# The bias of the last 64 query rows: masks for two key blocks at once in an attention and MLP kernel

## The chip, the cores and the metric

One core of a Trainium2 chip runs the whole program. The metric is the device time of one execution in microseconds. Three runs of the kernel before took 797.27, 798.25 and 798.29 us; the median is 798.25 us.

## The reference

Attention with 4 batches, 8 heads, 576 positions and head size 64, with a bias that a small network makes of the distance, followed by a two-layer MLP on 2304 rows:

```
scores = scale * q @ k.T                      # (4, 8, 576, 576)
x      = log1p(|i - j|) / log1p(max(i, 1))
h      = relu(x * w1 + b1)                    # 32 hidden
bias   = h @ w2                               # one 576 x 576 table per head
attn   = softmax(scores + bias);  o = attn @ v
y      = relu(o @ w_in) ** 2 @ w_out          # 512 -> 2048 -> 512
```

The bias doesn't depend on the batch, so its 8 tables are computed once.

## The kernel before, in words

**Query chunks.** The 576 query rows are four chunks of 128 and a tail chunk of 64 (`TAIL = 4`). `chunks` puts the tail first. A unit of attention is a batch, a pair of heads `hp` and a chunk. In a tail unit the two heads of the pair share the 128 partitions: the even head's 64 rows below, the odd head's above. The first 8 units are the tail units of two batches, then come the units of chunks 0 to 3 of these batches, then the other two batches.

**The bias.** Each hidden unit is a ramp, so for a query row the bias over keys is a sum of slopes and offsets of those hidden units that are active. For a block of 32 keys (`jb`, 18 of them) and a chunk, `bias_mask` (L361) compares the distances with thresholds `theta` on VectorE (DVE): 128 partitions are 4 keys by 32 hidden units, the free axis 8 groups by 128 query rows, f16. `bias_sum` (L378) multiplies each of the 8 masks by `wmov`, which holds w1*w2 and b1*w2 in two f16 parts, into one PSUM bank `bb`: 128 rows, 8 groups x (slope or offset) x 8 heads x 4 keys. ScalarE (ACT) scales the offsets out of PSUM (L392, for the tail L403), DVE multiplies the slopes by `xc`, the chunk's matrix x (L393, L404), GpSimd (POOL) adds both into the table in SBUF (L398, L405).

**The tail before.** A mask holds the 64 tail rows twice, in the lower and upper 64 columns: by a window with a repeat (L373), or for the six blocks whose bit is set in `MD` by a half mask (L369) that ACT copies (L375). The product gives all 8 heads in both halves; then two half-height ACT and DVE instructions take the even heads from the lower 64 partitions and the odd heads from the upper ones (L403, L404). Each of the 18 blocks takes 16 matmuls.

**Attention.** `scores` (L410): PE makes 576 scores into `sp` (L428, one PSUM buffer); DVE adds the bias and takes the maximum in one instruction (L434) and frees `sp`; ACT exponentiates (L439). `transposes` and `values` follow (L484, L487, L502), with copies out of PSUM by ACT. The `bb` tiles share four PSUM buffers with these ("aux"), masks have three buffers (`MB`), and `xc` has two: the tail's and the next chunk's. `load_xc` (L114) issues the load from SP and then scales the matrix on ACT (L121).

**The order.** The program is written with due counts: `bias_upto(n)` works off the list of (chunk, block) items, `K0` and `B1` say how many are due between the loads of the first batch's heads, `BO` how many beside each unit. A scheduler then places the instructions of each engine by its own estimate of times; the order that results is fixed and each engine works through its own list. SP issues the loads: constants, the tail's xc, then k, q and v of eight (batch, pair) groups, seven loads each, and then the xc of chunk 0.

Of the kernel before, what the change touches and what calls it, by code (L numbers as in the profile page):

```python
# [79 lines left out]
def attention_then_relu2_mlp(ctx: ExitStack, tc: tile.TileContext, q, k, v, cols, w_in, w_out, psi, xmat, dist, out):  # L80
# [279 lines left out]

    def bias_mask(ic, jb):  # L361
        m = prep.tile([128, 8, 128], F16, name="mask", tag="mask", bufs=MB)
        dup = ic == TAIL and (MD >> jb) & 1
        w = 64 if dup else 128
        base = sdist[:, 128 * ic + 548 - 32 * jb:]
        if ic < TAIL or dup:
            win = bass.AP(tensor=base.tensor, offset=base.offset, ap=[base.ap[0], [4, 8], [1, w]])
            th = theta[:, 128 * ic:128 * ic + w].unsqueeze(1)
            DVE.tensor_tensor(out=m[:, :, :w], in0=win, in1=th.to_broadcast([128, 8, w]), op=ALU.is_ge)  # L369
# [8 lines left out]
    def bias_sum(ic, jb):  # L378
        m = mask_t.pop((ic, jb))
        bb = ps.tile([128, 512], F32, name="bb", tag="aux", bufs=4)  # L380
        for r in range(8):
# [4 lines left out]
        xv = xc_t[ic][:, 32 * jb:32 * jb + 32].rearrange("p (g j) -> p g j", j=4).unsqueeze(1)
        bv = bb.rearrange("p (g a h j) -> p a h g j", g=8, a=2, h=H)
        tv = t.rearrange("p h (g j) -> p h g j", j=4)
        sv = s.rearrange("p h (g j) -> p h g j", j=4)
        js = slice(32 * jb, 32 * jb + 32)  # L390
# [499 lines left out]
```

## Time and profile before

| | |
|---|---|
| median of three runs | 798.25 us |
| profiled execution, its own time | 797.97 us |
| its span | 796.2 us |
| PE busy | 723.5 us, 91% |
| DVE busy | 574.5 us, 72% |
| ACT busy | 456.5 us, 57% |
| POOL busy | 186.4 us, 23% |

The span runs from the first to the last instruction of the profile. PE is the tensor engine (PEld its weight loads), SP the engine that issues the DMAs. A busy PE isn't PE at its peak. In the chain of waits, the work that ended last followed backwards, PE has 50% of the span, DVE 19%, ACT 8%, DMA 7% and the issuing on SP 6%.

### The profile page before, as it was taken

How to read it: one execution, taken by the hardware profiler on the slowest of the kernel's cores; microseconds unless marked ns; L12 is line 12 of the kernel's file. 1: busy time of each engine (PE TensorE's matmuls, PEld its weight loads, DVE VectorE, ACT ScalarE, POOL GpSimd, SP SyncE). 2: the span in 40 equal slices, each digit the busy share in tenths (PEclk: the TensorE clock that was granted, in tenths of full speed). 3: DMA queues.
4: the chain of work that ended last, by engine and by line, in shares of the span. 5: the costliest groups of instructions: out<-in, count | busy, mean ns of one | idle time of the engine just before them, and what ended most of it. 6: DMA issues, size and time to landing. Idle time of an engine off the chain costs nothing.

```text
span 796.2 us, 17616 instructions
## 1 busy us (share of the span) xinstructions
PE 723.5 (91%) x7094; PEld 571.7 (72%) x7094; DVE 574.5 (72%) x1215; ACT 456.5 (57%) x940; POOL 186.4 (23%) x295
## 2 busy tenths in 40 slices
PE   5499999999988999979889899999989999999992
PEld 5456778787756676656677677878768887888881
DVE  7867778785666678898897979784845576557661
ACT  5757777777655678888676656664442233224220
POOL 1444333232210023342223324250400021000000
PEclk7869999999989999999999999999999999999997
DMA  7610000000376522301231143001010001000100
GB/s 203 191 60 18 3 16 2 3 2 2 105 239 232 189 85 85 111 28 54 80 107 54 67 146 107 28 22 59 26 54 1 1 1 54 1 1 1 54 2 27
DMA packets 27990, 50.14 MB, mean 63 GB/s; under 512 B 5252, under 2 KB 13444, under 8 KB 27908
## 3 DMA queue, kind: packets, MB, share of 16 engines
q1 hardware_dynamic: 27908, 49.01, 18.8%
q8 instruction: 56, 0.92, 0.5%
q14 instruction: 26, 0.21, 0.1%
HBM read 43.23 MB, written 5.77 MB: 62 GB/s over the span
## 4 chain that ended last, share of the span: by engine, by line
PE 50%; DVE 19%; ACT 8%; DMA 7%; SPq 6%; issue 5%; POOL 3%; DVEq 0%; ACTq 0%; POOLq 0%
PE y L766 16%; PE ha L717 8%; PE sp L428 7%; PE px L502 6%; PE hb L717 5%; PE pp L484 4%; PE bb L383 4%; DMA stage<-in_w_in 3%; DVE t L434 3%; ACT p L439 2%; SPq L150 2%; SPq L151 2%; DVE area L618 2%; DVE gl L747 1%; DVE wa L185 1%
## 5 line engine op out<-in xcount | busy, mean ns | idle before, releaser
L766 PE MATMUL y<-w,gh 128*128 128x512 f32 x576 | 177.9, 401 | 2.5 <-ACT gh L746 1.3
L717 PEld LDWEIGHTS <-area 128*128 128x128 f16 x1680 | 147.4, 99 | 42.5 <-issue 15.3
L439 ACT ACTIVATE p<-t,negm 128x576 f32<-128x576 f32 x144 | 111.2, 775 | 27.0 <-DVE negm L434 26.8
L434 DVE CUSTOM_DVE_ANT_0 t<-sp,area 128x576 f32<-128x576 f32 x144 | 104.1, 752 | 30.0 <-PE sp L428 21.3
L766 PEld LDWEIGHTS y<-w,gh 128*128 128x128 f32 x576 | 105.9, 190 | 24.9 <-ACT gh L746 2.9
L428 PE MATMUL sp<-k,q 64*128 64x288 f32 (+1 forms) x640 | 108.2, 447 | 15.0 <-DVE negm L434 11.4
L717 PE MATMUL ha<-area 128*128 128x256 f16 (+1 forms) x960 | 106.3, 266 | 9.0 <-DVE area L734 4.9
L766 PE MATMUL y<-w,gl 128*128 128x512 f32 x288 | 107.5, 397 | 1.1 <-DVE gl L747 1.1
L502 PE MATMUL px<-pt,v 128*64 128x128 f32 (+1 forms) x1600 | 96.6, 267 | 3.5 <-DVE xT L507 2.0
L485 ACT COPY pt<-pp 128x512 f32<-128x512 f32 x144 | 79.7, 582 | 32.0 <-PE pp L484 31.9
L502 PEld LDWEIGHTS px<-pt,v 128*64 128x64 f32 x1600 | 79.2, 137 | 19.7 <-issue 8.2
L484 PE MATMUL pp<-ident,p 128*128 128x128 f32 x576 | 84.5, 283 | 5.5 <-ACT pt L485 2.4
L428 PEld LDWEIGHTS sp<-k,q 64*128 64x128 f32 (+1 forms) x640 | 55.9, 182 | 41.1 <-DVE negm L434 15.3
L717 PE MATMUL hb<-area 128*128 128x256 f16 (+1 forms) x720 | 79.9, 262 | 1.4 <-DVE area L618 0.9
L484 PEld LDWEIGHTS pp<-ident,p 128*128 128x128 f32 x576 | 62.0, 142 | 22.8 <-issue 7.4
L398 POOL TENSOR_TENSOR area<-bt,bt 128x256 f32<-128x256 f32 x72 | 53.2, 763 | 81.9 <-DVE bt L393 81.9
L383 PE MATMUL bb<-wmov,mask 128*128 128x64 f16 x1440 | 52.6, 199 | 14.3 <-DVE bt L404 11.0
L766 PEld LDWEIGHTS y<-w,gl 128*128 128x128 f32 x288 | 53.8, 189 | 13.6 <-DVE gl L747 2.2
L383 PEld LDWEIGHTS <-mask 128*128 128x128 f16 x1440 | 48.2, 102 | 21.3 <-DVE bt L404 11.8
L369 DVE TENSOR_TENSOR mask<-sdist,theta 128x1024 f16<-128x1024 f16 (+1 forms) x78 | 49.7, 669 | 9.4 <-PE bb L383 9.4
L615 POOL TENSOR_TENSOR area<-xT 128x512 f32<-128x512 f32 (+1 forms) x17 | 22.8, 1344 | 143.2 <-DVE area L618 143.2
L747 DVE TENSOR_TENSOR gl<-area,gh 128x512 fp32r<-128x512 f32 (+1 forms) x40 | 30.2, 776 | 24.1 <-ACT gh L746 17.2
(153 smaller groups left out, 945.9 us busy)
## 6 DMA issues: line engine op xcount, KB each, us to landing
stage<-in_w_in SPq DMA_DIRECT2D x32, 512.0 KB, 4.2
stage<-in_w_out SPq DMA_DIRECT2D x16, 512.0 KB, 3.5
v<-in_v SPq DMA_DIRECT2D x16, 320.0 KB, 3.8
out<-o SPq DMA_DIRECT2D x18, 256.0 KB, 2.0
q<-in_q SPq DMA_DIRECT2D x32, 128.0 KB, 3.3
k<-in_k SPq DMA_DIRECT2D x16, 160.0 KB, 3.7
k<-in_k SPq DMA_DIRECT2D x16, 144.0 KB, 3.7
xc<-in_xmat SPq DMA_DIRECT2D x5, 288.0 KB, 3.6
```

The costliest lines, as they stand in the source:

```text
L369: DVE.tensor_tensor(out=m[:, :, :w], in0=win, in1=th.to_broadcast([128, 8, w]), op=ALU.is_ge)
L383: PE.matmul(bb[:, 64 * (7 - r):64 * (8 - r)], lhsT=m[:, r], rhs=wmov[:, n], start=(n == 0), stop=(n == 1))
L398: POOL.tensor_tensor(out=dst, in0=tw, in1=sw, op=ALU.add)
L428: mm = PE.matmul(out_t[to, x, :HALF], lhsT=qt[rows, cols], rhs=kt[rows, k0:k0 + HALF], start=True, stop=True)
L434: DVE.tensor_tensor_reduce(out=t.rearrange("p (x n) -> p x n", x=2), in0=sp[:, :, :HALF], in1=bias.rearrange("p (x n) -> p x n", x=2), sca ...
L439: ACT.activation(out=p[:, S * n:S * n + S], in_=t, func=AF.Exp, bias=negm[:, n:n + 1], scale=-1.0, accum_out=sums[:, 2 * ic + n:2 * ic + n ...
L484: PE.transpose(pp[:, 128 * c:128 * c + 128], p[:, k0:k0 + 128], ident)
L485: ACT.copy(pt[:, 4 * h:4 * h + 4], pp.rearrange("p (c m) -> p c m", c=4))
L502: PE.matmul(px[64 * h:64 * h + 64, :w], lhsT=vt[:, c, h], rhs=src, start=(c == 0), stop=(c == 4))
L717: PE.matmul(h[:, s, :w], lhsT=a, rhs=x, start=(k == 0), stop=(k == 5))
L747: DVE.tensor_tensor(out=gl, in0=g, in1=gh.bitcast(F32), op=ALU.subtract)
L766: PE.matmul(y, lhsT=a[:, slot, o:o + 128], rhs=x, start=((n, P) in firsts and f == 0 and m == 0), stop=((n, P) in lasts and f == 1 and m = ...
```

## The change

A mask of the tail now holds the 64 rows against two neighbouring key blocks, one in each half of its 128 columns (a window with a step of 32 in place of the repeat); `bias_mask` takes block pairs, 9 of them, and `MD` with its copies on ACT is gone. The weights `ab` are ordered with the even heads first. `bias_sum` multiplies each half of a mask by the even heads' weights into the lower 64 partitions and by the odd heads' into the upper ones, 64 rows by 32 columns each, 64 matmuls for a pair; then one ACT, one DVE and one POOL instruction of full height finish 64 keys. `K0`, `B1` and the calls of `bias_upto` count pairs in place of blocks. Chunks 0 to 3 are computed as before, with the heads' order put right in the view that POOL reads.

```diff
-B1 = (2, 13, 8)
+B1 = (2, 5, 8)
-MD = 37449
-K0 = 2
+K0 = 1
...
-            eng.tensor_scalar(out=ab[:, n], in0=col[:, 2:10], scalar1=(w1, b1)[n], scalar2=8.0, op0=ALU.mult, op1=ALU.mult)
+            eng.tensor_scalar(out=ab[:, n].rearrange("p (e h) -> p e h", e=2), in0=col[:, 2:10].rearrange("p (h e) -> p e h", e=2), scalar1=(w1, b1)[n], scalar2=8.0, op0=ALU.mult, op1=ALU.mult)
...
     def bias_mask(ic, jb):
...
-            win = bass.AP(tensor=base.tensor, offset=base.offset, ap=[base.ap[0], [4, 8], [0, 2], [1, 64]])
+            base = sdist[:, 128 * ic + 548 - 32 * (jb + 1):]
+            win = bass.AP(tensor=base.tensor, offset=base.offset, ap=[base.ap[0], [4, 8], [32, 2], [1, 64]])
             th = theta[:, 512:].unsqueeze(1).unsqueeze(1).to_broadcast([128, 8, 2, 64])
-            DVE.tensor_tensor(out=m.rearrange("p g (r i) -> p g r i", r=2), in0=win, in1=th, op=ALU.is_ge)
-        if dup:
-            ACT.copy(m[:, :, 64:], m[:, :, :64])
+            out = m.rearrange("p g (x i) -> p g x i", x=2)
+        DVE.tensor_tensor(out=out, in0=win, in1=th, op=ALU.is_ge)
...
     def bias_sum(ic, jb):
...
         else:
-            for r in range(2):
-                rows = slice(64 * r, 64 * r + 64)
-                bw = bb[rows].rearrange("p (g a h e j) -> p a e h g j", g=8, a=2, h=HP, e=2)
-                ACT.activation(out=sv[rows, :HP], in_=bw[:, 1, r], func=AF.Identity, scale=bscale[rows])
-                DVE.tensor_tensor(out=tv[rows, :HP], in0=bw[:, 0, r], in1=xv[rows].to_broadcast([64, HP, 8, 4]), op=ALU.mult)
-            POOL.tensor_tensor(out=bias_t[:, 8::9, js], in0=t[:, :HP], in1=s[:, :HP], op=ALU.add)
+            wv = wmov.rearrange("p n (a e y) -> p n e a y", a=2, e=2)
+            for x in range(2):
+                for r in range(8):
+                    o = 256 * x + 32 * (7 - r)
+                    for n in range(2):
+                        for e in range(2):
+                            PE.matmul(
+                                bb[64 * e:64 * e + 64, o:o + 32].rearrange("p (a y) -> p a y", a=2),
+                                lhsT=m[:, r, 64 - 64 * x:128 - 64 * x], rhs=wv[:, n, e], start=(n == 0), stop=(n == 1),
+                            )
+            xv = xc_t[ic][:, 32 * jb:32 * jb + 64].rearrange("p (g j) -> p g j", j=4).unsqueeze(1)
+            bv = bb.rearrange("p (g a h j) -> p a h g j", g=16, a=2, h=HP)
...
+            ACT.activation(out=sv.rearrange("p h (g j) -> p h g j", j=4), in_=bv[:, 1], func=AF.Identity, scale=bscale)
+            DVE.tensor_tensor(out=tv.rearrange("p h (g j) -> p h g j", j=4), in0=bv[:, 0], in1=xv.to_broadcast([128, HP, 16, 4]), op=ALU.mult)
+            POOL.tensor_tensor(out=bias_t[:, 8::9, 32 * jb:32 * jb + 64], in0=tv, in1=sv, op=ALU.add)
...
-    todo = [(ic, jb) for ic in chunks for jb in range(NJB)]
+    todo = [(ic, jb) for ic in chunks for jb in range(0, NJB, 2 if ic == TAIL else 1)]
...
-    bias_upto(NJB)
+    bias_upto(NJB // 2)
     load_xc(chunks[1])
...
-            bias_upto(NJB * (n + 1) + BO[r])
+            bias_upto(NJB // 2 + NJB * n + BO[r])
```

The lines of the new kernel are shifted: the scaling of xc is L120 there (L121 before), the tail's product, activation and add L411, L410 and L412, chunk 0's activation and product L388 and L389, the reduction L441 (L434), the exponential L446 (L439).

The scheduler also places other work anew. ACT at the end of the tail's bias, before (`bt` are the scaled offsets, `xc` the chunk's matrix, `p` the exponentials; in brackets the engines or load queues that a row waits for):

```order
L403 ACTIVATE bt_723<-bb,small 64x128 [waits DVE_49]
L392 ACTIVATE bt_788<-bb,small 128x256 [waits PE_49,Pool_49]
L392 ACTIVATE bt_812<-bb,small 128x256 [waits PE_49,Pool_49]
L439 ACT_TABLE_LOAD
L439 ACTIVATE p,sums<-t,negm 128x576 [waits DVE_49] x2
L121 ACTIVATE xc<-xc,small 128x576 [waits DMAHW4_49]
L439 ACTIVATE p,sums<-t,negm 128x576 [waits DVE_49]
L121 ACTIVATE xc<-xc,small 128x576 [waits DMAHW5_49]
L392 ACTIVATE bt_848<-bb,small 128x256 [waits PE_49,Pool_49]
```

And now the same place on ACT:

```order
L410 ACTIVATE bt_641<-bb,small 128x256 [waits PE_49,Pool_49]
L410 ACTIVATE bt_713<-bb,small 128x256 [waits PE_49,Pool_49]
L120 ACTIVATE xc<-xc,small 128x576 [waits DMAHW4_49]
L410 ACTIVATE bt_835<-bb,small 128x256 [waits PE_49,Pool_49]
L388 ACTIVATE bt_922<-bb,small 128x256 [waits PE_49,Pool_49]
L388 ACTIVATE bt_946<-bb,small 128x256 [waits PE_49,Pool_49]
L388 ACTIVATE bt_970<-bb,small 128x256 [waits PE_49,Pool_49]
L120 ACTIVATE xc<-xc,small 128x576 [waits DMAHW5_49,DVE_49]
L388 ACTIVATE bt_1006<-bb,small 128x256 [waits PE_49,Pool_49]
L446 ACT_TABLE_LOAD
L446 ACTIVATE p,sums<-t,negm 128x576 [waits DVE_49]
```

The scaling of chunk 0's xc (the wait for DMAHW4) stood behind all of the tail's activations and two exponentials; now it stands ahead of the ninth pair's activation (`bt_835`). The second scaling stands ahead of the first exponential.

DVE at the first reduction of attention (`t,negm`), before:

```order
L369 TENSOR_TENSOR mask<-sdist,theta 128x1024 [waits PE_49]
L404 TENSOR_TENSOR bt_696<-bb,xc 64x128 [waits Activation_49]
L404 TENSOR_TENSOR bt_722<-bb,xc 64x128 [waits Activation_49]
L369 TENSOR_TENSOR mask<-sdist,theta 128x1024 [waits DVE_49,PE_49]
L434 ISA t,negm<-sp,area 128x576 [waits Pool_49]
L434 ISA negm 128x1
L369 TENSOR_TENSOR mask<-sdist,theta 128x1024 [waits DVE_49,PE_49]
L434 ISA t,negm<-sp,area 128x576 [waits PE_49]
```

And now:

```order
L411 TENSOR_TENSOR bt_834<-bb,xc 128x256 [waits Activation_49]
L372 TENSOR_TENSOR mask<-sdist,theta 128x1024 [waits DVE_49,PE_49]
L389 TENSOR_TENSOR bt_921<-bb,xc 128x256 [waits Activation_49]
L372 TENSOR_TENSOR mask<-sdist,theta 128x1024 [waits DVE_49,PE_49]
L441 ISA t,negm<-sp,area 128x576 [waits Pool_49]
L441 ISA negm 128x1
L389 TENSOR_TENSOR bt_945<-bb,xc 128x256 [waits DVE_49,Activation_49]
```

Between the tail's last product and the first reduction there was one mask; now there are two masks and a product of chunk 0.

DVE at the MLP's start, from the first pair's c to the second pair's reading of ha (`wa` and `stage` are a weight on its way into two parts), before:

```order
L734 SCALAR_TENSOR_TENSOR c<-ha,small,s 128x512
L186 SCALAR_TENSOR_TENSOR wa<-stage,wa 128x512
L735 SCALAR_TENSOR_TENSOR c<-hb,small,c 128x512
L183 TENSOR_SCALAR wa<-wa 128x512
L736 SCALAR_TENSOR_TENSOR c<-hb,small,c 128x512
L184 TENSOR_SCALAR wa<-wa 128x512
L185 SCALAR_TENSOR_TENSOR wa<-stage,wa 128x512
L186 SCALAR_TENSOR_TENSOR wa<-stage,wa 128x512
L733 SCALAR_TENSOR_TENSOR area<-ha,small,area 128x512
L734 SCALAR_TENSOR_TENSOR area<-ha,small,area 128x512
```

And now:

```order
L741 SCALAR_TENSOR_TENSOR c<-ha,small,s 128x512
L742 SCALAR_TENSOR_TENSOR c<-hb,small,c 128x512
L182 TENSOR_SCALAR wa<-wa 128x512
L743 SCALAR_TENSOR_TENSOR c<-hb,small,c 128x512
L183 TENSOR_SCALAR wa<-wa 128x512
L182 TENSOR_SCALAR wa<-wa 128x512
L184 SCALAR_TENSOR_TENSOR wa<-stage,wa 128x512
L183 TENSOR_SCALAR wa<-wa 128x512
L185 SCALAR_TENSOR_TENSOR wa<-stage,wa 128x512
L184 SCALAR_TENSOR_TENSOR wa<-stage,wa 128x512
L185 SCALAR_TENSOR_TENSOR wa<-stage,wa 128x512
L740 SCALAR_TENSOR_TENSOR area<-ha,small,area 128x512
```

Between the first pair's last c and the second pair's area from ha there were three weight steps; now there are seven, and one fewer ahead.

## Rows read from the trace of the kernel before

**Rows 1.** The page: busy time and share of each engine; POOL's adds of chunks.

```profile
PE 723.5 (91%) x7094; PEld 571.7 (72%) x7094; DVE 574.5 (72%) x1215; ACT 456.5 (57%) x940; POOL 186.4 (23%) x295
...
L398 POOL TENSOR_TENSOR area<-bt,bt 128x256 f32<-128x256 f32 x72 | 53.2, 763 | 81.9 <-DVE bt L393 81.9
```

**Rows 2.** Stretches: length, PE, PEld, DVE, ACT, POOL busy, granted clock, DMA, GB/s.

```profile
13.67:18.09 4.42, 4.42 (x80) 4.26 (x79) 4.14 (x10) 2.33 (x7) 0.96 (x1) 0.51 0.79 224
18.09:35.50 17.41, 8.18 (x241) 7.49 (x240) 15.86 (x45) 12.54 (x33) 8.79 (x15) 0.99 0.64 187
35.50:52.08 16.58, 12.27 (x108) 7.71 (x109) 10.23 (x24) 9.19 (x18) 5.81 (x11) 0.50 0.39 119
...
52.08:67.41 15.33, 15.33 (x288) 11.16 (x286) 12.18 (x28) 10.96 (x29) 9.32 (x14) 1.00 0.01 2
67.41:92.42 25.01, 22.16 (x364) 16.86 (x363) 19.66 (x50) 19.23 (x50) 9.78 (x14) 1.00 0.05 15
```

**Rows 3.** Timeline of DVE: start, duration in us, instruction, idle time before it.

```profile
39.05 0.76 DVE L434 CUSTOM_DVE_ANT_0 t<-sp,area 128x576 f32<-128x576 f32 x1
...
45.39 0.76 DVE L434 CUSTOM_DVE_ANT_0 t<-sp,area 128x576 f32<-128x576 f32 x1 [2.46 <-ACT xc L121]
...
46.07 1.08 DVE L393 TENSOR_TENSOR bt<-bb,xc 128x256 f32<-128x256 f32 x3
```

**Rows 4.** Timeline of ACT, 38 to 45 us.

```profile
38.88 1.28 ACT L439 ACT_TABLE_LOAD   x1
40.17 0.78 ACT L439 ACTIVATE p<-t,negm 128x576 f32<-128x576 f32 x1
...
44.56 0.78 ACT L121 ACTIVATE xc<-xc,small 128x576 f32<-128x576 f32 x1 [0.73 <-DMA xc<-in_xmat]
```

**Rows 5.** Timeline of SP, the two loads of xc after all k, q, v.

```profile
40.92 0.90 SPq L116 DMA_DIRECT2D xc<-in_xmat  x2
```

**Rows 6.** Groups by shape, 13 to 38 us: busy us, mean ns.

```profile
L403 ACT ACTIVATE bt<-bb,small 64x128 f32<-64x128 f32 x36 | 12.4, 360 | 7.9 <-POOL area L405 3.9 <-PE bb L383 2.8 <-DVE bt L404 0.4
...
L404 DVE TENSOR_TENSOR bt<-bb,xc 64x128 f32<-64x128 f32 x36 | 9.8, 286 | 1.2 <-ACT bt L403 0.8
...
L369 DVE TENSOR_TENSOR mask<-sdist,theta 128x512 f16<-128x512 f16 x5 | 2.0, 409 | 0.0
```

**Rows 7.** The tile mask: ns least, median and most, first and last start.

```profile
L369 DVE TENSOR_TENSOR mask<-sdist,theta x78: 406/685/885, 10.9 to 174.5; 128x1024 f16<-128x1024 f16 x72, 128x512 f16<-128x512 f16 x6
L373 DVE TENSOR_TENSOR mask<-sdist,theta x12: 673/689/797, 11.2 to 30.6; 128x1024 f16<-128x1024 f16 x12
```

**Rows 8.** Groups by shape, 46 to 60 us, instructions of the full height.

```profile
L392 ACT ACTIVATE bt<-bb,small 128x256 f32<-128x256 f32 x10 | 4.6, 470 | 4.4 <-PE bb L383 2.9 <-POOL area L398 1.5
L393 DVE TENSOR_TENSOR bt<-bb,xc 128x256 f32<-128x256 f32 x11 | 4.3, 417 | 1.0 <-ACT bt L392 1.0
```

**Rows 9.** Timeline of PE: small matmuls.

```profile
13.67 4.42 PE L383 MATMUL bb<-wmov,mask 128*128 128x64 f16 x80 [3.33 <-DVE wmov L356]
19.37 1.57 PE L383 MATMUL bb<-wmov,mask 128*128 128x64 f16 x48 [1.28 <-DVE bt L404]
...
57.26 0.80 PE L502 MATMUL px<-pt,v 128*64 128x64 f32 x20
```

**Rows 10.** Timeline: the third load of xc and its scaling.

```profile
69.44 0.33 SPq L116 DMA_DIRECT2D xc<-in_xmat  x1
...
72.17 0.78 ACT L121 ACTIVATE xc<-xc,small 128x576 f32<-128x576 f32 x1 [0.98 <-DMA xc<-in_xmat]
```

**Rows 11.** Timeline of PE: scores and first transposes.

```profile
39.87 2.25 PE L428 MATMUL sp<-k,q 64*64 64x288 f32 x8 [0.73 <-DVE negm L434]
...
51.07 1.71 PE L428 MATMUL sp<-k,q 64*64 64x288 f32 x6
...
53.18 0.64 PE L484 MATMUL pp<-ident,p 128*128 128x128 f32 x4
...
59.97 1.19 PE L428 MATMUL sp<-k,q 64*64 64x288 f32 x8
```

**Rows 12.** Timeline of PE at the MLP's start.

```profile
407.10 2.79 PE L717 MATMUL ha<-area 128*128 128x256 f16 x24 [1.40 <-DVE area L734]
```

More of the change, by code (lines that the diff above doesn't have):

```diff
@@ L362, in bias_mask @@
         m = prep.tile([128, 8, 128], F16, name="mask", tag="mask", bufs=MB)
[L363 to L369, printed above, removed]
-        else:
-            win = bass.AP(tensor=base.tensor, offset=base.offset, ap=[base.ap[0], [4, 8], [0, 2], [1, 64]])
+        if ic < TAIL:
+            base = sdist[:, 128 * ic + 548 - 32 * jb:]
+            win = bass.AP(tensor=base.tensor, offset=base.offset, ap=[base.ap[0], [4, 8], [1, 128]])
+            th = theta[:, 128 * ic:128 * ic + 128].unsqueeze(1).to_broadcast([128, 8, 128])
+            out = m
+        else:
+            base = sdist[:, 128 * ic + 548 - 32 * (jb + 1):]
+            win = bass.AP(tensor=base.tensor, offset=base.offset, ap=[base.ap[0], [4, 8], [32, 2], [1, 64]])
             th = theta[:, 512:].unsqueeze(1).unsqueeze(1).to_broadcast([128, 8, 2, 64])
-            DVE.tensor_tensor(out=m.rearrange("p g (r i) -> p g r i", r=2), in0=win, in1=th, op=ALU.is_ge)
-        if dup:
-            ACT.copy(m[:, :, 64:], m[:, :, :64])
+            out = m.rearrange("p g (x i) -> p g x i", x=2)
+        DVE.tensor_tensor(out=out, in0=win, in1=th, op=ALU.is_ge)
         mask_t[ic, jb] = m
@@ L380, in bias_sum @@
         bb = ps.tile([128, 512], F32, name="bb", tag="aux", bufs=4)
-        for r in range(8):
-            for n in range(2):
-                PE.matmul(bb[:, 64 * (7 - r):64 * (8 - r)], lhsT=m[:, r], rhs=wmov[:, n], start=(n == 0), stop=(n == 1))
         t = prep.tile([128, H, 32], F32, name="bt1", tag="bt1", bufs=BB)
         s = prep.tile([128, H, 32], F32, name="bt2", tag="bt2", bufs=BB)
[L386 to L390, printed above, removed]
-        if ic < TAIL:
+        if ic < TAIL:
+            for r in range(8):
+                for n in range(2):
+                    PE.matmul(bb[:, 64 * (7 - r):64 * (8 - r)], lhsT=m[:, r], rhs=wmov[:, n], start=(n == 0), stop=(n == 1))
+            xv = xc_t[ic][:, 32 * jb:32 * jb + 32].rearrange("p (g j) -> p g j", j=4).unsqueeze(1)
+            bv = bb.rearrange("p (g a h j) -> p a h g j", g=8, a=2, h=H)
+            tv = t.rearrange("p h (g j) -> p h g j", j=4)
+            sv = s.rearrange("p h (g j) -> p h g j", j=4)
             ACT.activation(out=sv, in_=bv[:, 1], func=AF.Identity, scale=bscale)
@@ L396, in bias_sum @@
             dst = bass.AP(tensor=dst.tensor, offset=dst.offset, ap=[dst.ap[0], [9 * S, HP], [odd, 2], [1, 32]])
-            tw, sw = (y.rearrange("p (h e) j -> p h e j", e=2) for y in (t, s))
+            tw, sw = (y.rearrange("p (e h) j -> p h e j", e=2) for y in (t, s))
             POOL.tensor_tensor(out=dst, in0=tw, in1=sw, op=ALU.add)
         else:
-            for r in range(2):
-                rows = slice(64 * r, 64 * r + 64)
-                bw = bb[rows].rearrange("p (g a h e j) -> p a e h g j", g=8, a=2, h=HP, e=2)
-                ACT.activation(out=sv[rows, :HP], in_=bw[:, 1, r], func=AF.Identity, scale=bscale[rows])
-                DVE.tensor_tensor(out=tv[rows, :HP], in0=bw[:, 0, r], in1=xv[rows].to_broadcast([64, HP, 8, 4]), op=ALU.mult)
-            POOL.tensor_tensor(out=bias_t[:, 8::9, js], in0=t[:, :HP], in1=s[:, :HP], op=ALU.add)
+            wv = wmov.rearrange("p n (a e y) -> p n e a y", a=2, e=2)
+            for x in range(2):
+                for r in range(8):
+                    o = 256 * x + 32 * (7 - r)
+                    for n in range(2):
+                        for e in range(2):
[5 more added lines that the diff above has]
+            bv = bb.rearrange("p (g a h j) -> p a h g j", g=16, a=2, h=HP)
+            tv = t.rearrange("p (h x) y -> p h (x y)", x=2)
+            sv = s.rearrange("p (h x) y -> p h (x y)", x=2)
+            ACT.activation(out=sv.rearrange("p h (g j) -> p h g j", j=4), in_=bv[:, 1], func=AF.Identity, scale=bscale)
+            DVE.tensor_tensor(out=tv.rearrange("p h (g j) -> p h g j", j=4), in0=bv[:, 0], in1=xv.to_broadcast([128, HP, 16, 4]), op=ALU.mult)
+            POOL.tensor_tensor(out=bias_t[:, 8::9, 32 * jb:32 * jb + 64], in0=tv, in1=sv, op=ALU.add)
     p_t, pt_t, sum_t = {}, {}, {}
```

## The prediction

> **What bounds the kernel now.** I read the page first: PE is busy 91% of the span and nothing else over 72% [rows 1], so a change pays only where PE stands still. Then the engines by stretch of the first 92 us [rows 2]. The reader is to see three stages there. From 13.67 to 35.5 us (two rows) DVE is busy 20.0 of 21.8 us and PE 12.6: the tail chunk's masks and products hold the start. From 35.5 to 52.08 us PE runs at a granted clock of 0.50, 1.2 GHz, with gaps. From 52.08 to 67.41 us PE is busy all 15.33 us at 1.00, and in the next 25.01 us it stands still 2.85 us (25.01 less 22.16). After that the order of work is the same in both kernels down to the MLP's start, so I take it that what is lost or won by 92 us reaches the end nearly whole.
>
> Then the timeline of the second stage, engine by engine [rows 3 to 5]. Before, tail unit 0 is reduced on DVE at 39.05 and exponentiated at 40.17, unit 2 follows at 45.39, paced by score matmuls of 2.25 us a unit at the low clock [rows 11]. SP issues loads without a pause until the second xc load at 40.92, behind the k, q and v of all eight groups; ACT scales it at 44.56, when it lands. Two of the three exponentials stand ahead of that scaling on ACT.
>
> **The tail bias itself.** Before: 12 masks of 0.69 us, 6 half masks of 0.41 and 36 products of 0.29 on DVE, 8.3 + 2.5 + 10.4 = 21.2 us; now 9 masks of 0.69 and 9 products of 128x256 at 0.42, 10.0 us [rows 6 to 8]. ACT's 36 activations of 0.36, 13.0 us, and its six copies become 9 x 0.47 = 4.2; POOL's 18 adds of 128x128 become 9 of 128x256. So DVE would give back 11 us if nothing else held the stage.
>
> PE pays: 288 matmuls of 128x128 weights on 64 columns become 576 of 128x64 weights on 32. No row shows that form. Nearest are the old form, 48 in 1.57 us (33 ns each) at the full clock and 80 in 4.42 (55 ns) at half, and the px matmuls with the same 128x64 weights, but f32 and 64 columns, 20 in 0.80 (40 ns) [rows 9]. Below lies half the old form, 16 ns. The clock rose at about 18 us before, after 4.4 us of unbroken matmuls [rows 2]; the new stage starts 0.28 us later (its first mask is whole, not half), at 13.95, and I let it have the same 4.4 us at 55 ns (80 matmuls), then 496 at 33 to 40 ns, 16.4 to 19.8 us. It ends at 34.8 to 38.2 us, with 16 ns at 26 or, at one price throughout, 23 us; I take 36.5, nearest to the old form. That costs nothing as long as something else holds the stage beyond it, and something does.
>
> The Trainium skill speaks against the smaller matmuls. "TensorEngine Tiling (Array Packing)", section Performance Considerations, says that a matmul has a floor of about 60 cycles and no factor should be taken from a dimension that is already small, and its section Restrictions and Gotchas that column tiling excludes the fast weight load; "TensorE: Matmul & The Clock Gate", section LDWEIGHTS, puts an ordinary load at its columns over 1.2 in ns, 53 ns for 64. By that, 576 x 53 ns (an estimate) would end the stage at 44.5 us. The px rows with 64-column weights go at 40 ns a pair, so here the trace contradicts the 53; 44.5 would still just be covered by the wait below, half a microsecond from where rival C begins, and half of C's chance rests on it.
>
> **The wait that takes the place.** On ACT the scaling of chunk 0's xc, which needs the load issued at 40.92, now stands ahead of the ninth pair's activation; before it stood behind two exponentials (the rows of the order shown with the change). SP's order of the 60 loads ahead of it is unchanged, each issued in about 0.6 us, so I keep 44.56. Queued behind it on ACT: the ninth pair, chunk 0's first activations, the second xc scaling and all exponentials. Who waits: DVE's ninth product, POOL's ninth add, by it the first reduction, and SP's next xc load, which needs the tail's xc buffer back. Worked out:
> ACT scaling 44.56 + 0.78 = 45.34; ninth activation + 0.47 = 45.8; its product + 0.42 = 46.2; POOL's add + 0.76 = 47.0 [rows 1, 4, 8].
> DVE then has in order a mask, a product, a mask and the first reduction: a mask at 0.69 and a product at 0.36 when they follow closely (three in 1.08), so 46.2 + 0.69 + 0.36 + 0.69 = 47.9, and the reduction of 0.76 is done at 48.7. Before it began at 39.05: 8.8 us late [rows 3].
> The next xc load leaves at 46.2 and, as the one at 69.44 that ACT took at 72.17, needs 2.7: 48.9. Scaling 0.78, one activation 0.47, the table load 1.28: first exponential 51.4 to 52.2. Before 40.17: 11.2 us late [rows 4, 10].
> PE stands still from about 38 to 46.9 (block 3's mask), so I give it the low clock again: blocks 3 and 4 at 0.88 each (16 of the 80 in 4.42), unit 1's scores 2.25, to 51.0; it rises as before some 5 us after PE becomes busy; blocks 5 to 7 to 52.7; unit 2's scores 1.19; the first transposes at 54.2. Before they began at 53.18, with units 3 and three quarters of 4 already scored [rows 9, 11]. So PE is 1.0 us late and owes 1.75 x 1.19 = 2.1 us: 3.1.
>
> **What is lost and caught up after.** From there DVE has a backlog (two reductions of 0.76, two products and a mask, 3.1 us), and blocks 8 and 9 need PSUM buffers that it frees about 0.6 us after PE could start: 3.7. Against it, the 2.85 us in which PE stood still before, between 67.41 and 92.42. They have the same cause: the next xc load could only leave at 69.44, and ACT stood before its scaling for 0.98 us [rows 2, 10]. That scaling comes one activation later in the new order, so part goes: at least none, at most all 2.85; I take 1.0, since the load itself stays. Net + 2.7 us; the bounds are 3.1 - 2.85 = + 0.25 and 3.7 + 1.5 = + 5.2, the 1.5 for a backlog that runs on a unit longer (two reductions at 0.76).
>
> The scheduler also moved the MLP's start: before the second unit's products from ha, DVE now has three more weight steps, and y's first eight matmuls stand before the third ha. PE waited 1.40 us there for DVE [rows 12]. Bounds - 1.4 (the wait goes) and + 1.4 (it doubles); I take 0, as PE has y's work to fill the gap. The reordered weights ab and the table of due counts (2, 5, 8) move no time of their own: the same two instructions on 8 columns, and half as many items.
>
> The profiled execution took 797.97 us, 0.28 under the median 798.25. 797.97 + 2.7 = 800.7.
>
> **Rivals.** A: caught up. If DVE's halved work leaves no backlog, PE runs without a gap from 54.2 to 92 and takes back all 2.85: 798.2. For it: every product of chunk 0 needed the same load before too (first one at 46.07), so only scores and exponentials were ahead. Against: DVE is busy 12.18 of 15.33 us in the stage after [rows 2], so its slack there is no more than the backlog of 3.1.
> B, faster: ACT isn't held, because the load is there when the eighth pair is done. Everything from 45.8 on moves up with it; it breaks even once the load lands 2.7 us sooner, and if it landed with the tail's end, 38.2, 6.4 us sooner, the time would be 797.97 + 2.7 - 6.4 = 794.3. For it: the halved stage really ends by then. Against: SP's issues fill the time to 40.92 with no idle to remove.
> C, much slower: the new matmuls keep the half clock's price or double a half-clock pair. From 54 ns each they pass 45 us (13.95 + 31.1), and each 10 ns more adds 5.8: at 76 ns, 813. Against: PE is busier than before in that stretch, and before it was granted 1.00 there.
> D: the MLP's start decides: its 1.40 us go, and the catching up stops half way between forecast and A, 797.97 + 1.5 - 1.4 = 798.1.
>
> **Chances.** Forecast 0.57, A 0.24, B 0.10, D 0.05, C 0.04. The likeliest time is 800.7, the forecast's own range 799.9 (below that it is A) to 803.2. The range that holds 8 in 10 leaves out B and C: 797.0, A less most of the MLP's 1.4, to 803.8, the upper bound 5.2 taken with part of it caught up and part of the MLP's 1.4. A measurement here can tell 0.2%, 1.6 us. Slower than that: forecast and C, 0.61. Within: A and D, 0.29. Faster: B, 0.10.
>
> **What would show it.** Right: ACT idle until about 44.5 before the xc scaling with the load as releaser, the ninth activation behind it, first reduction near 48, first exponential near 51.5, first transposes near 54; DVE idle some 8 us from about 37. Wrong: an exponential before 45; bb matmuls of the tail still running at 44; first transposes under 53; or the distance at 92 us under 1 us. If the tail matmuls take over 40 ns at the full clock, that step is wrong without changing the sum.

## The result, and the profile after

The changed kernel took 801.15 us (median of 11 runs, 797.70 to 805.88); the kernel before 797.27 (11 runs, 795.02 to 799.39). The ratio is 1.0059, with a 95% interval from 1.0039 to 1.0078: slower by 4.7 us by the ratio, 3.9 by the medians. The forecast was 800.7, its range 797.0 to 803.8. The profiled execution, 805.88 us, is the slowest of the eleven, which matters below.

The page of the changed kernel first, busy time by engine [rows 1], then four stretches with the same columns as [rows 2]:

```profile
PE 726.5 (90%) x7382; PEld 577.6 (72%) x7382; DVE 564.9 (70%) x1179; ACT 443.8 (55%) x907; POOL 185.6 (23%) x286
```

```profile
20.00:30.00 10.00, 8.37 (x308) 8.15 (x306) 4.60 (x11) 1.93 (x5) 3.61 (x5) 0.50 0.59 160
30.00:40.00 10.00, 4.43 (x107) 4.13 (x103) 1.62 (x3) 0.44 (x1) 0.78 (x2) 0.50 0.49 145
40.00:50.00 10.00, 0.00 (x0) 0.00 (x0) 0.47 (x2) 1.64 (x4) 0.00 (x0) 0.50 0.56 175
50.00:60.00 10.00, 8.25 (x123) 5.96 (x124) 10.00 (x19) 6.95 (x15) 7.67 (x9) 0.81 0.11 31
```

DVE is 9.6 us lighter and ACT 12.7. Yet from 40 to 50 us PE does nothing at all and DVE and ACT nearly nothing: the saved work has become a hole. The waits from 30 to 60 us (who waited for whom, us in total, times, longest) name its head:

```profile
POOL area L412 <- DVE bt L411: 21.6, 3, 18.3
ACT xc L120 <- DMA xc<-in_xmat: 17.9, 1, 17.9
DVE bt L411 <- ACT bt L410: 15.5, 1, 15.5
...
PE bb L383 <- DVE mask L372: 14.7, 1, 14.7
```

Read from the second line on: ACT waited for a transfer, DVE for ACT, POOL and PE for DVE. The timeline of all engines through the hole, which answers [rows 3 to 5, 9, 11]:

```profile
13.88 8.76 PE L402 MATMUL bb<-wmov,mask 128*64 128x32 f16 x316 [3.85 <-DVE wmov L355]
...
45.13 5.18 SPq L115 DMA_DIRECT2D xc<-in_xmat  x2
48.37 0.78 ACT L120 ACTIVATE xc<-xc,small 128x576 f32<-128x576 f32 x1 [17.93 <-DMA xc<-in_xmat]
49.05 0.45 ACT L410 ACTIVATE bt<-bb,small 128x256 f32<-128x256 f32 x1
49.53 0.42 DVE L411 TENSOR_TENSOR bt<-bb,xc 128x256 f32<-128x256 f32 x1 [15.54 <-ACT bt L410]
51.62 0.74 DVE L441 CUSTOM_DVE_ANT_0 t<-sp,area 128x576 f32<-128x576 f32 x1
52.74 0.78 ACT L120 ACTIVATE xc<-xc,small 128x576 f32<-128x576 f32 x1 [1.08 <-DVE bt L389]
53.89 1.28 ACT L446 ACT_TABLE_LOAD   x1
55.19 0.78 ACT L446 ACTIVATE p<-t,negm 128x576 f32<-128x576 f32 x1
57.98 0.66 PE L491 MATMUL pp<-ident,p 128*128 128x128 f32 x4
```

The scaling of chunk 0's xc stands ahead of the ninth pair's activation, and both wait for a load that SP issued at 45.13. The first reduction comes at 51.62 instead of 39.05, the first exponential at 55.19 instead of 40.17. The load itself is 4.2 us later than before [rows 5], though SP's order is the same: five of the issues ahead of it took 1.1 to 3.1 us, before three took 1.3 to 1.8. In experiment e5, with these loads and narrow matmuls too, it left at 41.39. So most of the 3.8 us by which the scaling starts later (48.37 against 44.56) belongs to this execution. Whether all does isn't shown: the four kernels traced here with wide matmuls in the tail (before, e4, e8, e10) have three such long issues each, the seven with narrow ones five or more. Why isn't settled.

The tail's groups by shape, 13 to 38 us, answer to [rows 6 to 8]; the last two lines below are the third xc load and its scaling [rows 10]:

```profile
L402 PE MATMUL bb<-wmov,mask 128*64 128x32 f16 x576 | 16.2, 214 | 7.0 <-DVE wmov L355 3.8 <-issue 3.1
...
L372 DVE TENSOR_TENSOR mask<-sdist,theta 128x1024 f16<-128x1024 f16 x9 | 6.2, 692 | 10.0 <-PE bb L402 10.0
...
L411 DVE TENSOR_TENSOR bt<-bb,xc 128x256 f32<-128x256 f32 x8 | 3.3, 417 | 0.0
```

```profile
76.86 0.33 SPq L115 DMA_DIRECT2D xc<-in_xmat  x1
...
79.70 0.78 ACT L120 ACTIVATE xc<-xc,small 128x576 f32<-128x576 f32 x1
```

DVE's masks now wait 10.0 us for PE: the tail is paced by the narrow matmuls, 16.2 us for 576, 28 ns each on average. By the trace they start in twos: of the 575 distances from one start to the next, 283 are under 8 ns and 283 about 50 (46 to 54), so that a couple takes 53 ns. In the program, neighbours write to the two halves of the output partitions in turn. The wait before the third scaling, 0.98 us before, is gone.

How the lateness travels is read from DVE's 144 reductions, one for each unit of attention, in order. The 20th and the last, of before:

```profile
96.51 0.75 DVE L434 CUSTOM_DVE_ANT_0 t<-sp,area 128x576 f32<-128x576 f32 x1
...
386.26 0.75 DVE L434 CUSTOM_DVE_ANT_0 t<-sp,area 128x576 f32<-128x576 f32 x1
```

and of after:

```profile
101.69 0.75 DVE L441 CUSTOM_DVE_ANT_0 t<-sp,area 128x576 f32<-128x576 f32 x1
...
393.37 0.74 DVE L441 CUSTOM_DVE_ANT_0 t<-sp,area 128x576 f32<-128x576 f32 x1
```

The same starts for all kernels with a profile that is compared here, as us ahead (-) or late (+) of before's:

| reduction | before | after | e1 | e5 | e6 | e4 | e8 | e11 |
|---|---|---|---|---|---|---|---|---|
| 1st | 39.05 | +12.6 | -3.8 | -4.1 | -3.8 | +11.8 | +1.8 | +1.9 |
| 5th | 54.48 | +11.6 | +6.5 | 0.0 | -5.0 | +9.2 | -1.6 | +0.7 |
| 20th | 96.51 | +5.2 | +0.1 | -0.9 | -10.9 | +1.4 | -8.5 | -5.2 |
| 80th | 234.39 | +5.2 | -0.1 | -1.4 | -10.6 | +1.1 | -9.3 | -5.9 |
| 100th | 285.27 | +6.9 | +0.7 | +0.6 | -10.4 | +1.7 | -7.1 | -6.2 |
| 144th | 386.26 | +7.1 | +0.7 | +0.6 | -10.1 | +4.0 | -7.1 | -5.9 |
| from there to the span's end | 409.9 | 410.7 | 410.2 | 407.7 | 408.5 | 418.9 | 409.0 | 408.4 |

What stands at the 20th reduction reaches the last within 2 us, except in e4 (in e10 and e14, not in the table, within 4). More than half of the first 12.6 us is gone before it, but not only because a backlog was worked off: the scheduler also rearranged the work between, which the lists of the order shown with the change leave out. Ahead of the 5th reduction 179 of chunk 0's `bb` matmuls stand now, before 128; only at the 20th has PE done the same work again, and from about 95 us on the orders agree down to the MLP's start. So PE's account is drawn up there: the stretch from the tail's last matmul to the 20th reduction, for before, after, e8 and e6 in this order, 853 matmuls each (columns as in [rows 2]):

```profile
34.36:96.51 62.15, 54.82 (x853) 39.81 (x851) 46.63 (x109) 42.23 (x103) 27.83 (x43) 0.86 0.14 40
33.27:101.69 68.42, 51.30 (x853) 38.96 (x855) 48.15 (x106) 39.95 (x100) 28.44 (x39) 0.85 0.18 53
34.71:88.00 53.29, 48.39 (x853) 36.78 (x851) 48.68 (x109) 40.18 (x102) 29.27 (x42) 1.00 0.15 44
32.48:85.59 53.11, 50.30 (x853) 38.71 (x855) 47.52 (x106) 39.53 (x99) 28.21 (x39) 0.96 0.19 58
```

PE stands idle 17.1 us there after the change, 7.3 before: 9.8 us more. The 853 matmuls keep it busy 3.5 us less, since by the trace only 5.7 us of them ran at the granted 0.50, before 12.6; and the tail ended 1.1 us earlier. That gives the 5.2. From the 5th to the 20th reduction alone, after and e5:

```profile
66.06:101.69 35.63, 35.54 (x616) 27.22 (x616) 32.49 (x76) 27.94 (x73) 16.35 (x24) 1.00 0.04 11
54.50:95.66 41.16, 38.06 (x663) 29.25 (x661) 33.13 (x80) 30.74 (x78) 19.20 (x29) 1.00 0.03 10
```

PE's 2.85 us of idle time before [rows 2] have become 0.09. In e5, where the order is before's again but for a few instructions, 3.10 are left.

### The profile page after: what moved, and what is told of

Read it like the earlier page. It is cut to its first block, busy times and chain, and to the rows that moved or that the text cites. A ratio compares the mean times of both kernels' runs of the same rounds, so it can differ in the third digit from the quotient of the medians.

```text
span 804.1 us, 18110 instructions
## 1 busy us (share of the span) xinstructions
PE 726.5 (90%) x7382; PEld 577.6 (72%) x7382; DVE 564.9 (70%) x1179; ACT 443.8 (55%) x907; POOL 185.6 (23%) x286
## 4 chain that ended last, share of the span: by engine, by line
PE 53%; DVE 18%; DMA 8%; ACT 7%; issue 5%; SPq 5%; POOL 2%; DVEq 0%; ACTq 0%; POOLq 0%
PE y L773 18%; PE ha L724 8%; PE sp L435 7%; PE px L509 6%; PE hb L724 5%; PE pp L491 5%; PE bb L383 3%; DMA stage<-in_w_in 3%; DVE t L441 3%; DMA stage<-in_w_out 2%; ACT p L446 2%; DVE area L625 1%; SPq L149 1%; SPq L150 1%; DVE gl L754 1%
## 5 line engine op out<-in xcount | busy, mean ns | idle before, releaser
L446 ACT ACTIVATE p<-t,negm 128x576 f32<-128x576 f32 x144 | 111.1, 774 | 26.4 <-DVE negm L441 26.2
L441 DVE CUSTOM_DVE_ANT_0 t<-sp,area 128x576 f32<-128x576 f32 x144 | 103.7, 751 | 26.2 <-PE sp L435 25.0
L435 PE MATMUL sp<-k,q 64*128 64x288 f32 (+1 forms) x640 | 104.5, 438 | 9.7 <-DVE negm L441 7.1
L372 DVE TENSOR_TENSOR mask<-sdist,theta 128x1024 f16<-128x1024 f16 x81 | 56.1, 728 | 16.1 <-PE bb L402 10.0
L383 PE MATMUL bb<-wmov,mask 128*128 128x64 f16 x1152 | 41.5, 197 | 15.3 <-DVE mask L372 14.7
L383 PEld LDWEIGHTS <-mask 128*128 128x128 f16 x1152 | 37.6, 100 | 20.6 <-DVE mask L372 15.4
```

The source lines that it names most:

```text
L372: DVE.tensor_tensor(out=out, in0=win, in1=th, op=ALU.is_ge)
L435: mm = PE.matmul(out_t[to, x, :HALF], lhsT=qt[rows, cols], rhs=kt[rows, k0:k0 + HALF], start=True, stop=True)
L441: DVE.tensor_tensor_reduce(out=t.rearrange("p (x n) -> p x n", x=2), in0=sp[:, :, :HALF], in1=bias.rearrange("p (x n) -> p x n", x=2), sca ...
L446: ACT.activation(out=p[:, S * n:S * n + S], in_=t, func=AF.Exp, bias=negm[:, n:n + 1], scale=-1.0, accum_out=sums[:, 2 * ic + n:2 * ic + n ...
```

## The experiments

Theory A is the forecast's: ACT, in order, is held by the scaling of an xc that comes late. The rivals: B, the narrow matmuls cost the time; C, it is lost later, in DVE's backlog or at the MLP's start.

**e1: the first scaling's load early.** In the changed kernel:

```diff
+    load_xc(chunks[1])
     scale_xc(chunks[0])
     bias_upto(K0)
...
     bias_upto(NJB // 2)
-    load_xc(chunks[1])
```

> The changed kernel with one line moved: the load of chunk 0's xc is issued behind the first head's k, q and v instead of behind all 60 of them, and its scaling on ACT then stands ahead of the first tail pair. The scaling of chunk 1's xc, whose load still goes out behind the 60 loads, stays ahead of the first exponential. Theory A (ACT, in order, is held by the scaling of a late xc): the ninth tail pair is no longer held, the first reduction comes at 37 to 40 us instead of 51.6, but the first exponential waits for the second xc, about 45 to 49 us instead of 55.2; the time falls by 2 to 5 us against the changed kernel's 801.2, so 796 to 799. Rival B (the 512 narrow matmuls of the tail cost it, on PE or through the clock): no change, 800 to 802. Rival C (the loss is later, at DVE's backlog or the start of the MLP): the first reduction comes early and the time stays at 800 to 802.

Measured: 798.41 us, before beside it 797.02, ratio 1.0008 (0.9983 to 1.0034). Its interval lies wholly under the changed kernel's. The timeline of e1:

```profile
35.21 0.74 DVE L441 CUSTOM_DVE_ANT_0 t<-sp,area 128x576 f32<-128x576 f32 x1
...
48.21 0.77 ACT L120 ACTIVATE xc<-xc,small 128x576 f32<-128x576 f32 x1 [12.52 <-DMA xc<-in_xmat]
...
50.66 0.78 ACT L446 ACTIVATE p<-t,negm 128x576 f32<-128x576 f32 x1
```

The first reduction moves from 51.62 to 35.21. Then the second scaling, which also stands ahead of the first exponential, is held in the first one's place, 12.52 us. Narrow matmuls and the MLP's order are as in the changed kernel: B and C expected no gain. A holds, though the first exponential, expected at 45 to 49, came at 50.66.

**e5: ACT's order put back.**

```diff
-        if ic != chunks[0]:
+        if ic not in chunks[:2]:
             scale_xc(ic)
...
+        if s == 0:
+            scale_xc(chunks[1])
```

(The first exponential and the two scalings are also pinned to their places in the program.)

> The changed kernel with only ACT's order put back to that of the kernel before: the scaling of chunk 0's xc stands behind the first exponential, that of chunk 1's xc behind the score units that come ahead of it in the program. Loads, matmuls and masks as changed. Theory A: the first reduction at 37 to 40 us, the first exponential at 38 to 42 us, the second behind the landing of xc (44 to 49 us); time as the kernel before's or a little under, 795 to 798. Rival B (narrow matmuls): 800 to 802. Rival C (loss later): 800 to 802 with an early first exponential.

Measured: 798.52 us, ratio 1.0025 (0.9997 to 1.0053): 0.34% under the changed kernel's ratio, 2.7 us, though the two intervals just overlap; half a microsecond above the upper end expected. The scheduler then also placed DVE's and PE's later work nearly as before, so e5 doesn't give the price of ACT's order alone. The timeline of e5:

```profile
34.92 0.74 DVE L443 CUSTOM_DVE_ANT_0 t<-sp,area 128x576 f32<-128x576 f32 x1
...
44.81 0.77 ACT L120 ACTIVATE xc<-xc,small 128x576 f32<-128x576 f32 x1 [7.22 <-DMA xc<-in_xmat]
45.61 1.09 DVE L391 TENSOR_TENSOR bt<-bb,xc 128x256 f32<-128x256 f32 x3 [7.64 <-ACT xc L120]
```

The tail is done 4 us earlier than before, and DVE then stands 7.64 us for the xc, which lands as late as before (44.81 against 44.56). Even with ACT's old order the change gains nothing while that load stays where it is.

**e6: no xc wait at all.** e1, and the second scaling kept at its place in the program:

```diff
+        ins = ACT.activation(out=xc_t[ic], in_=xc_t[ic], func=AF.Identity, scale=bscale)
+        if ic == chunks[2]:
+            tc.keep_in_program_order(ins)
```

> The changed kernel with both: chunk 0's xc loaded behind the first head's k, q and v, and the scaling of chunk 1's xc held behind the work ahead of it in the program. Theory A: no wait for an xc is left ahead of the first exponentials; first reduction 37 to 40 us, first exponential 38 to 42 us, first transposes at 47 to 51 us instead of 58.0; time 792 to 796, under the kernel before. Rival B: 800 to 802. Rival C: 800 to 802 with early transposes.

Measured: 786.79 us, ratio 0.9875 (0.9832 to 0.9918): faster than both kernels, and by more than expected. The timeline of e6:

```profile
11.47 0.78 ACT L120 ACTIVATE xc<-xc,small 128x576 f32<-128x576 f32 x1 [1.73 <-DMA xc<-in_xmat]
...
35.22 0.74 DVE L443 CUSTOM_DVE_ANT_0 t<-sp,area 128x576 f32<-128x576 f32 x1
...
37.88 0.78 ACT L448 ACTIVATE p<-t,negm 128x576 f32<-128x576 f32 x1
...
40.90 0.65 PE L493 MATMUL pp<-ident,p 128*128 128x128 f32 x4
```

The first transposes start at 40.90, 12.3 us ahead of before [rows 11], and 10.1 us of that are left at the last reduction. I had reckoned with the wait that the change made longer, not with the one that was in the kernel before already.

**e4: the order forced on the kernel before.** Its tail's last two blocks come behind load and scaling of chunk 0's xc:

```diff
-    bias_upto(NJB)
+    bias_upto(NJB - 2)
     load_xc(chunks[1])
+    bias_upto(NJB)
```

(with that scaling and the blocks' activations pinned.)

> The kernel before (its masks, wide matmuls and half activations) with ACT's order made that of the changed kernel: the scaling of chunk 0's xc ahead of the last two tail blocks' activations, and that of chunk 1's xc ahead of the first exponential. No narrow matmul. Theory A: first reduction at 46 to 50 us instead of 39.1, first exponential 49 to 55 us; 2 to 5 us slower than the kernel before, 799 to 802. Rival B: as the kernel before, 796 to 798. Rival C (DVE's backlog or the MLP's start in the changed code): as the kernel before.

Measured: 805.41 us, ratio 1.0117 (1.0073 to 1.0160). ACT's scaling waited 11.82 us, and the first reduction came at 50.84:

```profile
45.43 0.78 ACT L121 ACTIVATE xc<-xc,small 128x576 f32<-128x576 f32 x1 [11.82 <-DMA xc<-in_xmat]
...
50.84 0.75 DVE L438 CUSTOM_DVE_ANT_0 t<-sp,area 128x576 f32<-128x576 f32 x1
```

So the hold needs no narrow matmul. The size doesn't count: of the 13.0 us by which its profiled execution was late, 1.4 stood at the 20th reduction, and 9.0 came behind the last one; from about 349 us on the scheduler had also rearranged the work, the MLP's start included. e4 shows how the hole arises, not what it costs.

**e8: e6's two edits in the kernel before.**

```diff
+    load_xc(chunks[1])
     scale_xc(chunks[0])
...
     bias_upto(NJB)
-    load_xc(chunks[1])
```

(and the second scaling pinned as in e6.)

> The kernel before (its masks and wide tail matmuls) with both xc waits taken away as in e6: chunk 0's xc loaded behind the first head's k, q and v, the scaling of chunk 1's xc held behind the work ahead of it in the program. Theory A (the wait for xc had been the bound of the start in the kernel before too, and hid what the tail's change is worth): 787 to 794, of which the part above e6's 786.8 is the worth of the change without the wait; the first reduction stays at about 39 us (e6: 35.2), so 3 to 5 us over e6, 790 to 792. Rival D (the tail's change is worth nothing, all of e6's gain is the early xc): as e6, 785 to 788. Rival E (e6's gain needs the changed tail): as the kernel before, 795 to 798.

Measured: 790.32 us, before 797.88, ratio 0.9909 (0.9882 to 0.9936). Most of e6's gain comes with these two edits, which the old tail takes as well. The account above says how: of e8's 8.5 us at the 20th reduction, 6.4 are busy time saved on the same 853 matmuls and 2.4 idle time, less 0.35 for a tail that ends later. Before, the clock was granted at 0.50 from 35.1 to 52.2 us and 12.6 us of matmuls ran in it; in e8 it was at 1.00 from 22.2 us on. e6's 10.9 are 4.5 us of busy time, 4.5 of idle time, and 1.9 for a tail that ends earlier. What is left for the change itself is 0.34% between the two ratios, 2.7 us, with intervals that overlap; at the 20th reduction it is 2.4 us (8.5 against 10.9).

**e10: e6 with wide matmuls in the tail.** Sixteen of 128x128 weights on 64 columns a pair instead of 64 narrow ones; the tail's bias then takes wrong heads in half of its rows.

```diff
-            for x in range(2):
-                for r in range(8):
...
+            for r in range(8):
+                for n in range(2):
+                    PE.matmul(bb[:, 64 * (7 - r):64 * (8 - r)], lhsT=m[:, r], rhs=wmov[:, n], start=(n == 0), stop=(n == 1))
```

> e6 with 16 matmuls of 128x128 weights and 64 columns a pair in the tail instead of 64 of 64 columns and 32 (the tail's bias then takes the wrong heads in half of its rows; this is for the time alone). If the narrow matmuls set the tail stage (64 x 27 ns = 1.7 us a pair against 1.1 us of DVE), the stage's end comes 4 to 7 us earlier, the first reduction at 28 to 31 us, and the time is 780 to 784. If they are hidden, 785 to 788. The clock: if 128-column weights bring it up, the granted clock rises before 25 us as in the kernel before; if it stays at 0.50 until 35 us, not their shape but something else had raised it there.

Measured: 779.09 us, ratio 0.9764 (0.9731 to 0.9797), 1.1% under e6. The stretches of e10, and the timeline of its tail:

```profile
15.00:20.00 5.00, 4.55 (x93) 4.42 (x90) 5.00 (x10) 2.67 (x6) 3.40 (x3) 0.61 0.64 181
20.00:25.00 5.00, 2.78 (x74) 2.76 (x75) 5.00 (x10) 1.46 (x4) 4.59 (x5) 1.00 0.64 189
```

```profile
13.78 5.77 PE L400 MATMUL bb<-wmov,mask 128*128 128x64 f16 x112 [2.68 <-DVE wmov L357]
...
20.38 0.63 PE L400 MATMUL bb<-wmov,mask 128*128 128x64 f16 x16 [0.83 <-DVE bt L406]
```

Once no xc is waited for, the narrow matmuls bind: with 144 wide ones in place of the 576, e6 is some 8 us faster. How much of that is their number and how much the clock isn't separated. In the changed kernel itself that was under cover. With wide matmuls the granted clock reached 1.00 (2.4 GHz) by 20 us; with narrow ones it stayed at 0.50 (1.2 GHz) to the tail's end.

**e11: the same narrow matmuls, 16 in a row to one half of the output partitions.**

```diff
-            for x in range(2):
+            for x, e in ((0, 0), (0, 1), (1, 0), (1, 1)):
                 for r in range(8):
```

> e6 with the tail's narrow matmuls in another order: 16 in a row into the same 64 output partitions (the same half of the array's columns), then 16 into the other, instead of one to each half in turn. If two neighbours overlap because they lie in different halves, the 27 ns of one become up to 55 ns, a pair takes 3.5 us instead of 1.7, the tail stage ends 10 to 15 us later and the time is 795 to 802. If a narrow matmul takes 27 ns by itself, nothing changes: 785 to 788.

Measured: 791.60 us, ratio 0.9921 (0.9890 to 0.9953). The timeline of the tail, and a stretch within it:

```profile
13.89 24.32 PE L404 MATMUL bb<-wmov,mask 128*64 128x32 f16 x576 [3.68 <-DVE wmov L357]
```

```profile
30.00:35.00 5.00, 5.00 (x125) 5.00 (x123) 2.05 (x4) 0.95 (x2) 1.45 (x2) 0.50 0.65 192
```

One narrow matmul takes 42 ns here on average (24.32 us / 576) against 28 when the two halves take turns, and the stage ended at 38.2 us, some 6 later than in e6, not 10 to 15. The starts in the trace say more. The first matmuls of the tail start 53 ns apart; then each group of 16 has one distance under 8 ns (35 in all, as many as there are changes of half), five of about 27, and the rest 47 to 54. So within one half most matmuls take the 53 ns that a couple takes in the changed kernel, and time is saved about each change of half: neighbours in different halves do overlap, by half where they take turns. The new order also puts the two matmuls that add into the same columns side by side; but the distances don't alternate with that, so it isn't the reason. The short distance stands three matmuls ahead of the change, so a recorded start isn't the moment of the multiplying itself. PE was busy without a gap for 24.32 us and the clock was granted at 0.50 throughout.

**e12, e13, e14: can the clock be brought up?** e12 adds ten matmuls of 128x128 weights while PE waits for the tail; e13 adds eight wide ones ahead of each pair; e14 does both.

```diff
+        for _ in range(W2):
+            PE.matmul(pw[:, 256:272], lhsT=ones, rhs=r, start=True, stop=True)
...
+            for r in range(8):
+                PE.matmul(bb[:, 64 * (7 - r):64 * (8 - r)], lhsT=m[:, r], rhs=wmov[:, 0], start=True, stop=True)
```

> e6 with ten more matmuls (128x128 float32 weights, 16 columns, a result that nobody reads) in the time in which TensorE waits for the tail's weights, about 9 to 13.6 us, so that it comes to the tail busy. In e6 the narrow matmuls ran 20 us at a granted clock of 0.50. If the clock comes up before the tail and stays up under narrow matmuls, one takes about 14 to 20 ns instead of 27, the first reduction comes 4 to 8 us earlier (27 to 31 us) and the time is 779 to 784. If narrow matmuls of 64 columns don't hold the clock, it falls back or never rises, and the time is e6's, 785 to 788.

> e6 with eight matmuls of 128x128 weights and 64 columns ahead of each tail pair's 64 narrow ones, into the columns that these then overwrite (72 more in all; at half clock 8 x 55 ns = 0.44 us a pair). If wide weights bring the clock up, it rises within the tail as in e10, the pairs get shorter and the time is 780 to 786; if eight among 64 are too few, the clock stays at 0.50 to 35 us, the stage ends 4 us later (9 x 0.44) and the time is 788 to 792.

> e6 with both: the ten matmuls ahead of the tail and the eight wide ones ahead of each pair. If wide weights are what holds the clock, it is at 1.00 through the tail, a pair takes 8 x 33 ns + 64 x 14 to 20 ns = 1.2 to 1.5 us instead of 1.7, the first reduction comes at 27 to 32 us and the time is 779 to 784. If it falls all the same, 788 to 792 as by e13's worse case.

Measured, against 797.41 for before: e12 789.15 (0.9895, 0.9848 to 0.9942), e13 791.27 (0.9914, 0.9885 to 0.9944), e14 792.97 (0.9937, 0.9911 to 0.9964). Of e12 only the times are read. e12 and e14 lie about 1 us above the slower of the two ranges expected for each. Of e14, the added matmuls (ten, recorded as twenty), one pair, and a stretch:

```profile
10.52 4.45 PE L355 MATMUL pw<-ab,ones 128*128 128x16 f32 x20
...
26.59 0.61 PE L403 MATMUL bb<-wmov,mask 128*128 128x64 f16 x8
27.13 1.89 PE L409 MATMUL bb<-wmov,mask 128*64 128x32 f16 x64
```

```profile
25.00:30.00 5.00, 5.00 (x164) 4.75 (x160) 2.33 (x6) 0.95 (x2) 1.45 (x2) 0.50 0.61 167
```

The attempt failed: the clock stayed at 0.50 in e13 and e14, and the added matmuls only lengthened the tail. e6 remains the fastest version that computes the reference.

## Why the prediction was right

**The wait.** Right in kind, and in its steps once the landing is given. Counted from the start of the first scaling, forecast and measured: first reduction 3.3 us (47.9 - 44.56) and 3.25 (51.62 - 48.37); first exponential 6.8 to 7.6 and 6.82; first transposes 9.6 (54.2 - 44.56) and 9.61. Before, the same load had two exponentials ahead of it on ACT; taking the hold away (e1, e6) removes the loss. Two steps were off. "I keep 44.56" rests on issues of about 0.6 us each, and passed over the few long ones that decide when the load leaves. And the steps to the first transposes add up to 53.9 (52.7 + 1.19), not to 54.2.

**The sum.** +2.7 us forecast, 3.9 by the medians and 4.7 by the ratio (3.1 to 6.2): the size came out low. The terms were not right one by one, and that the median fits is in part luck. I let 1.0 of PE's 2.85 us of idle time be caught up; 2.8 were (0.09 left). The changed kernel is late by 5.2 at the 20th reduction. Without the late landing's 3.8, if all of it passes through, that is 1.4, where I had the whole 2.7 by 92 us; so some 4.2 were owed (1.4 + 2.8, an estimate) where I had 3.7. e4, whose scaling started 0.9 us later than before's, has 1.4 too.

A further 1.6 us came between the 80th and the 100th reduction, which no step of mine held. There the granted clock fell for a while; the same place in before and after (columns as in [rows 2]):

```profile
271.40:278.60 7.20, 6.59 (x74) 5.03 (x74) 4.39 (x18) 5.00 (x13) 0.00 (x0) 1.00 0.23 77
276.70:284.80 8.10, 7.48 (x60) 5.55 (x62) 3.81 (x16) 5.13 (x13) 0.00 (x0) 0.79 0.20 67
```

The seven traces with such a fall there (after, e1, e5, e8, e10, e13, e14) lose 1.9 to 2.7 us against before from the 90th to the 100th reduction, the three without it (e4, e6, e11) 0.5 to 0.7. The order of work is the same in all. Just ahead of it PE stood still for 0.93 of 3.70 us in after, but in e6 for 1.25 of 4.00 without a fall; what decides it isn't settled.

**The tail's own work.** DVE's 10.0 us for masks and products came out (9 x 0.692 + 9 x 0.417). The price of the narrow matmuls failed as a step: I let the clock rise after 4.4 us and then took 33 to 40 ns each; it stayed at 0.50 to the tail's end, and each took 28 ns on average even so. That the stage ended at 33.3 us, near the 36.5, is luck: two errors that nearly cancel. Under the wait it changed nothing, as forecast; e10 shows it as the next bound.

The 53 ns for a load of 64 columns that I drew from the Trainium skill, "TensorE: Matmul & The Clock Gate", section LDWEIGHTS, agree with the trace: 53 ns from one couple of matmuls to the next. What failed is the product 576 x 53, which sets the loads one behind the other. The Trainium skill's "TensorEngine Tiling (Array Packing)", Key Properties, says that different tiles load weights and multiply in parallel; the trace agrees, with two in 53 ns where neighbours lie in different halves and mostly one in 53 within a half, and I should have weighed that sentence. The Trainium skill's "TensorE: Matmul & The Clock Gate" also says in Part 1 that successive matmuls never start less than about 25 ns apart, however narrow; the mean of 28 ns agrees, the recorded starts, 283 of 575 under 8 ns apart, don't, and no run here settles it. The px matmuls of [rows 9] start in twos as well, 6 or 7 ns apart, the couples 58 apart but for one gap: their mean of 40 ns, which I set against the 53, was no price of a single one.

**The rivals.** A: nearly all of the 2.85 us was taken back, as it says, but more than 3.1 was owed. B would have needed an early landing; it came late. C's 54 ns was not reached. D: from the last reduction to the end after took 410.7 us and before 409.9, and the other seven kernels with the new start of the MLP (e1, e5, e6, e10, e11, e13, e14) took 407.7 to 410.6, so no cost of it is shown. In the place of the 1.40 us [rows 12] PE waits there for DVE's c and ACT's gh, as the timeline of after shows; over the whole MLP, by the pages, its waits before ha fell from 9.0 to 6.1 us while those before these y rose from 2.5 to 5.8:

```profile
409.08 2.79 PE L724 MATMUL ha<-area 128*128 128x256 f16 x24 [1.07 <-DVE c L741]
...
416.99 2.14 PE L773 MATMUL y<-w,gh 128*128 128x512 f32 x8 [3.15 <-ACT gh L753]
```

## What to carry to other kernels

Work taken from a stage that ends in a wait for a transfer moves the wait, not the end: find the transfer that the next stage needs, and move its issue before thinning the work ahead of it. On an engine that runs in order, look after every change for an instruction that waits on a load and now stands ahead of work that doesn't need it. Here one load moved up and one scaling pinned were worth 7.6 us to the old tail (e8) and some 14 to the new one (e6 against the changed kernel). Look at the granted clock beside the gaps, too: the larger part of e8's gain, 6.4 of 8.5 us, is matmuls that no longer run at 0.50.

## What the runs showed of the hardware

At the 1.2 GHz level, matmuls of 32 columns, each with a 64-column weight load, started in twos under 8 ns apart when neighbours wrote to different halves of the partitions, with 53 ns from one couple to the next (after, 28 ns each on average). With 16 in a row to one half, most started about 53 ns apart (e11, 42 on average, with the overlap about each change of half). And PE stayed at 0.50 through 24.32 us of unbroken narrow matmuls (e11) and through a tail of 21 us with wide ones mixed in and others ahead (e14), while with wide ones alone it had 1.00 by 20 us (e10). What decides it isn't settled here.
